# A fused attention and SwiGLU decode step: constant products in the first pass, and the last rows of W_O sent to half of the partitions

## The chip, the cores and the metric

The kernel runs on one core of a Trainium2 chip. The metric is the device time of one launch in microseconds. Before the change three runs gave 196.25, 196.48 and 198.06, so the median is 196.48 us. Lower is better. One further execution was taken with the hardware profiler; it took 196.53 us, of which 195.2 us lie between the first and the last instruction (the span).

## The reference

One decode step for a batch of 4, with one token of width 512 each:

```python
xn  = layernorm(x)                                  # x: 4 x 512
q   = xn @ wq                                       # 32 query heads of 128
k,v = last 4096 positions of the caches             # 8 key/value heads, 4 query heads share one
o   = softmax(q @ k.T * 128**-0.5) @ v
out = x + o @ wo + (silu(xn @ w_gate) * (xn @ w_up)) @ w_down
```

All tensors are bf16. The K and V windows together are 64 MiB, the five weight matrices about 13 MiB, and each byte is used once. The output is 4 x 512.

## The kernel before, in words

Five engines run their own instruction lists, written out by hand and tied by semaphores: TensorE (PE, with its weight loads as PEld), VectorE (DVE), ScalarE (ACT), GpSimd (POOL), and SyncE (SP), which issues all loads but that of x. The order of the loads is the order in which SP issues them: W_Q, W_gate, W_up, then for each of eight passes two halves of K and the whole of V, with W_down behind the first V, and at the end W_O in four pieces. There is one buffer for K, in two halves, and one for V. So a half of K waits until PE has transposed the same half of the pass before (line 264), and a V waits until the products with the V before have ended (line 269).

The start (lines 408 to 445) normalizes x, makes the queries, gate and up products, and ends in 14 constant products (`spin`), which multiply a tile of ones by a constant mask and whose result nobody reads.

A pass r (lines 521 to 539) handles one key/value head for all four batch rows. Each of the 128 partitions holds 128 positions, in 16 chunks of 8. PE transposes a chunk (L451), DVE or ACT copies it out of PSUM (L357, L299), and PE makes the scores two chunks later (L466). DVE then reduces maxima (L363, L365), PE transposes them (`maxima`, L473), DVE makes the shift from them (L368 to L372), PE adds the shift to the scores by a product (`shift`, L478), ACT takes the exponential (L302), and PE makes P·V (L487) and the denominators (L493). The signal that P·V has ended lets SP load the next V and DVE take the sums (L375, L376). `fin` (L500, L502) and `norm` (L380 to L385) of a pass run inside the next one. Between scores and maxima stand five constant products, between maxima and shift five, and behind P·V four, each group under `eng.If(r > 0)`, so that the first pass skips them.

The tail (lines 541 to 568) finishes the last pass, multiplies by W_down, and then by W_O. W_O lies with 32 rows on each partition: partition p holds rows 32p to 32p + 31. The attention result has another layout, with head dimension and quarter spread over the partitions, so four products with a selecting matrix `dr` (L551) permute it and DVE copies the result to OP (L401). The pieces of W_O are rows 0 to 21, 22 to 26, 27 to 29 and 30 to 31 of every partition (`WOS`). The first 22 rows go through `acc4` (L507), four rows side by side into four strips of PSUM, whose sums ACT copies to SBUF (L314) and PE adds by `acc` (L511) with a selecting matrix. The other rows go straight through `acc`, four products of 128 columns for a row. DVE and ACT copy the result out (L404, L317), and two stores end the kernel.

Of the kernel before, what the change touches and what calls it, by code (L numbers as in the profile page):

```python
# [10 lines left out]
def bass_parallel_sum__sliding_block_cached__swiglu_ffn__decode_kernel(  # L11
# [32 lines left out]
    SCALE = float(Dh) ** -0.5  # L44
    EPS = 1e-5
    OFF = -1.0e9
    WOS = (0, 22, 27, 30, 32)
    WOE = 22
    NR = HQ * Dh // 128

# [6 lines left out]
    WU = sb("wu_sb", [128, NC, F], BF16, 512)  # L57
    WD = sb("wd_sb", [128, NF, D], BF16, 512)
    WO = sb("wo_sb", [128, NR, D], BF16, 512)
    X = sb("x_sb", [B, D], BF16, 512)  # L60
    KT = sb("kT", [128, 4, CH, 128], BF16, 512)
    Qb = KT[:, 3].rearrange("p (a k) d -> p a (k d)", a=2)
# [22 lines left out]
    OT = sb("oT", [128, B, HKV + 1, REP, 4], BF16)  # L85

    OP = sb("oP", [128, NR, 32], BF16)
    S2 = sb("s2", [128, D], FP32)
    ex = S2[:, 0:F // 4]
    sel4 = sb("sel4", [128, B], FP32)  # L90
# [43 lines left out]
    acc_ps = ps_S[0][:, 0:HD]  # L134
    acc4_ps = ps_S[1]
    perm_ps = ps_kt[2][:, 0:B * NR]

    def sem(name):
        return nc.alloc_semaphore(name=name)
# [3 lines left out]
    d_wu = sem("d_wu")  # L143
    d_wd = sem("d_wd")
    d_out = sem("d_out")
    d_wo = [sem("d_wo%d" % q) for q in range(4)]
    d_k = [sem("d_k%d" % s) for s in range(2)]
    d_v = sem("d_v")
    s_go = sem("s_go")
# [29 lines left out]
    s_nrm = sem("s_nrm")  # L179
    s_pm = sem("s_pm")  # L180
    s_pc = sem("s_pc")
    s_e = sem("s_e")
    s_ec = sem("s_ec")
    s_acc = sem("s_acc")
# [6 lines left out]
    wu_ap = B_w_up.rearrange("(p c) n -> p c n", c=NC)  # L191
    wd_ap = B_w_down.rearrange("(p t) n -> p t n", t=NF)
    wo_ap = A_wo.rearrange("(p r) n -> p r n", r=NR)

    def kv_ap(cache, g, a, b):
        return cache[:, g, Sk - W:, :].rearrange("b (j t) d -> j b t d", j=NJ)[:, :, a:b, :]
# [62 lines left out]
    def on_sync(eng):  # L259
        H = NT // 2  # L260

        def load_k(g, h):
            if g > 0:
                eng.wait_ge(s_tr, NCH * (g - 1) + (h + 1) * NCH // 2)
            eng.dma_start(KB[:, h * H:(h + 1) * H, :], kv_ap(A_k_cache, g, h * H, (h + 1) * H)).then_inc(d_k[h], 16)

        def load_v(g):
            if g > 0:
                eng.wait_ge(s_pv, g)
            eng.dma_start(VB[:], kv_ap(A_v_cache, g, 0, NT)).then_inc(d_v, 16)  # L270

        def load_wo(n, a, b):
            eng.dma_start(WO[:, a:b, :], wo_ap[:, a:b, :]).then_inc(d_wo[n], 16)

        eng.dma_start(WQ[:], wq_ap).then_inc(d_wq, 16)
        eng.dma_start(WG[:], wg_ap).then_inc(d_wg, 16)
        eng.dma_start(WU[:], wu_ap).then_inc(d_wu, 16)
        for g in range(HKV):
            load_k(g, 0)
            load_k(g, 1)  # L280
            load_v(g)
            if g == 0:
                eng.dma_start(WD[:], wd_ap).then_inc(d_wd, 16)
        for q in range(4):
            load_wo(q, WOS[q], WOS[q + 1])
        eng.wait_ge(s_y[0], 1)
        eng.dma_start(out_ap[0], y[:, 0:D // 2]).then_inc(d_out, 16)
        eng.wait_ge(d_out, 32)
# [33 lines left out]
    def on_vector(eng):  # L322
        eng.wait_ge(d_x, 16)
        eng.tensor_reduce(st_sum[:], X[:], AX.X, ALU.add)  # L324
        eng.drain()
        eng.tensor_scalar(st_mean[:], st_sum[:], 1.0 / D, None, ALU.mult)
        eng.drain()
        eng.tensor_scalar(xc[:], X[:], st_mean[:, 0:1], None, ALU.subtract)
        eng.drain()
        eng.tensor_tensor(xsq[:], xc[:], xc[:], ALU.mult)  # L330
        eng.drain()
        eng.tensor_reduce(st_sum[:], xsq[:], AX.X, ALU.add)
        eng.drain()
        eng.tensor_scalar(st_var[:], st_sum[:], 1.0 / D, EPS, ALU.mult, ALU.add).then_inc(s_var, 1)
        eng.wait_ge(s_std, 1)
        eng.reciprocal(st_rstd[:], st_std[:])
        eng.drain()
        eng.tensor_scalar(xn[:], xc[:], st_rstd[:, 0:1], None, ALU.mult).then_inc(s_xn, 1)  # L338
        eng.wait_ge(s_xT, 1)
        eng.tensor_copy(XnT[:, :, 0:B], xT_ps.rearrange("p (c b) -> p c b", b=B)).then_inc(s_xnT, 1)  # L340
        eng.wait_ge(s_zero, 1)
        eng.tensor_copy(sel4b[:], sel4[:])
        eng.wait_ge(s_q, 1)
        eng.tensor_copy(Qb[:, 0], ps_S[0][:]).then_inc(s_qb, 1)
        eng.wait_ge(s_qt, 1)
        for j in range(2):
            eng.tensor_copy(QT[:, 0:HKV].rearrange("p (n j) (b h) -> p j n b h", j=2, b=B)[:, j],
                            qt_ps.rearrange("p (j h) (n b) -> p j n b h", j=2, n=4)[:, j, :, 0:B, :])
        eng.drain()

        eng.tensor_copy(QC[:], QT[:, 0])

        def group(r):
            for c in range(NCH):
                if c not in ACT_CH:
                    eng.wait_ge(s_tr, r * NCH + (c + 1))
                    eng.tensor_copy(KT[:, c % 4], kt_ps[c % 3]).then_inc(s_ev, 1)  # L357
                if c == 2:
                    norm(r)
                for q in range(NB):  # L360
                    if c == min(NCH - 1, (q + 1) * NCH // NB + 1):
                        eng.wait_ge(s_sc, r * NB + (q + 1))
                        eng.tensor_reduce(mx[:, q, :], ps_S[q][:].rearrange("p (t n) -> p n t", n=NH), AX.X, ALU.max)  # L363
            eng.drain()
            eng.tensor_reduce(m16[:], mx[:].rearrange("p q n -> p n q"), AX.X, ALU.max).then_inc(s_m, 1)  # L365
            eng.tensor_copy(QC[:], QT[:, bass.ds(r + 1, 1)].rearrange("p o n -> p (o n)"))
            eng.wait_ge(s_mt, r + 1)
            eng.tensor_tensor(junk[:], mT_ps, moff[:], ALU.add)  # L368
            eng.drain()
            eng.tensor_reduce(M[:], junk[:], AX.X, ALU.max)  # L370
            eng.drain()
            eng.scalar_tensor_tensor(CM[0:NH, :], neg[:], M[:, 0:1], coff[:], ALU.mult, ALU.add).then_inc(s_cm, 1)  # L372

            eng.wait_ge(s_pv, r + 1)
            eng.tensor_copy(Osb[:], O_ps)  # L375
            eng.tensor_reduce(dsum[:], den_ps.rearrange("p (t n) -> p n t", n=NH), AX.X, ALU.add).then_inc(s_dn, 1)  # L376

        def norm(r):
            eng.wait_ge(s_fin, r + 1)
            eng.reciprocal(den[:], D2_ps)  # L380
            eng.drain()
            eng.tensor_tensor(on[:], O2_ps, den[:], ALU.mult)
            eng.drain()
            o = OT[:, :, r] if isinstance(r, int) else OT[:, :, bass.ds(r, 1)].rearrange("p b o h q -> p b (o h) q")
            eng.tensor_tensor(o, on[:].rearrange("p (b h) -> p b h", b=B).unsqueeze(3).to_broadcast([128, B, REP, 4]),  # L385
                              dq[:].unsqueeze(1).unsqueeze(1).to_broadcast([128, B, REP, 4]), ALU.mult).then_inc(s_nrm, 1)

        eng.wait_ge(s_ex, 1)
        eng.tensor_scalar(ex, ex, 1.0, None, ALU.add)
        eng.drain()  # L390
        eng.reciprocal(ex, ex)
        eng.drain()
        eng.tensor_tensor(gs[:], gate_ps, ex, ALU.mult)
        eng.drain()
        eng.wait_ge(s_u, 1)
        eng.tensor_tensor(GUc, up_ps, gs[:], ALU.mult).then_inc(s_gu, 1)
        with eng.Fori(0, HKV) as r:
            group(r)
        norm(HKV)
        eng.wait_ge(s_pm, 1)  # L400
        eng.tensor_copy(OP[:, :, 0:B].rearrange("p r b -> p b r"), perm_ps.rearrange("p (b r) -> p b r", b=B)).then_inc(s_pc, 1)  # L401
        eng.wait_ge(s_acc, 1)
        for n in range(2):
            last = eng.tensor_copy(y[:, HD * n:HD * (n + 1)], acc_ps[32 * n:32 * n + B, :])  # L404
        last.then_inc(s_y[0], 1)

    def on_tensor(eng):
# [113 lines left out]
        with eng.Fori(0, HKV) as r:  # L521
            for c in range(NCH):
                transposes(r, c)
                if c == 2:
                    fin(r)
                if c >= 2:
                    scores(r, c - 2)
            scores(r, NCH - 2)
            scores(r, NCH - 1)
            with eng.If(r > 0):  # L530
                spin(5)
            maxima(r)
            with eng.If(r > 0):
                spin(5)
            shift(r)
            eng.wait_ge(d_v, r * 16 + 16)
            pv(r)
            with eng.If(r > 0):
                spin(4)

        fin(HKV)
        eng.wait_ge(s_gd, 1)
# [6 lines left out]
        eng.wait_ge(s_nrm, HKV + 1)  # L549
        for b in range(B):  # L550
            last = mm(perm_ps[:, NR * b:NR * (b + 1)], OT[:, b, 1:].rearrange("p k h q -> p (k h q)"), dr[:])  # L551
        last.then_inc(s_pm, 1)
        spin(2, 1)
        acc(ident[0:B, 0:B], X[:], True, False)
        eng.wait_ge(s_pc, 1)
        for q in range(4):
            eng.wait_ge(d_wo[q], 16)
            for e in range(WOS[q], WOS[q + 1]):
                if e < WOE:
                    last = acc4(e % 4, OP[:, e, :], WO[:, e, :], False, e >= WOE - 4)  # L560
                else:
                    last = acc(OP[:, e, 0:B], WO[:, e, :], False, e == NR - 1)
            if WOS[q + 1] == WOE:
                last.then_inc(s_e, 1)
            if q == 1:
                eng.wait_ge(s_ec, 1)
                acc(sel4[:], S2[:], False, False)
        last.then_inc(s_acc, 1)


# [34 lines left out]
```

## Time and profile before

| What | Value |
|---|---|
| median of three runs | 196.48 us (196.25 to 198.06) |
| the profiled execution | 196.53 us |
| its span | 195.2 us |
| PE busy | 161.9 us, 83% of the span |
| DVE busy | 108.8 us, 56% |
| ACT busy | 62.7 us, 32% |
| bytes read from HBM | 81.01 MB, 415 GB/s over the span |
| share of the loads' queue in the time of 16 transfer engines | 97.4% |
| mean granted PE clock | 0.956 |

Busy time is a mean over stages. A matmul's end is modelled, so that a busy PE is not PE at its peak. The 16 transfer engines share each load; a load has landed when all its parts have. The granted clock is the share of full speed that PE is given in a stretch of time.

### The profile page before, as it was taken

The numbers are of one execution on the slowest core, as the hardware profiler recorded it, in microseconds if no ns is written. First come the engines' busy times: TensorE is split into PE (matmuls) and PEld (weight loads), VectorE is DVE, ScalarE is ACT, GpSimd is POOL, SyncE is SP. The second block draws the span as 40 slices with busy tenths as digits, with TensorE's granted clock in tenths as the row PEclk, the third lists the DMA queues.
The fourth block names the chain that finished last, engine by engine and source line by source line (L and its number), as shares of the span: only waits on it lengthen the run. The fifth ranks groups of instructions, "written<-read, shape, count | busy, mean of one in ns | idle before, by whom it ended". The sixth has DMA issues, their size and how long they took to land.

```text
span 195.2 us, 7044 instructions
## 1 busy us (share of the span) xinstructions
PE 161.9 (83%) x3016; PEld 125.9 (65%) x3016; DVE 108.8 (56%) x224; ACT 62.7 (32%) x81; POOL 16.1 (8%) x55
## 2 busy tenths in 40 slices
PE   0038599855499999999999899979997999899994
PEld 0023169723499669947984698559855985698542
DVE  0252847831248828863893478347834783578341
ACT  2003106421026244513553064406440644064402
POOL 7763080000000000000000000000000000000000
PEclk9999699978559999999999999999999999999999
DMA  6999999999999999999999999999999999999992
GB/s 215 431 440 432 419 430 440 440 405 440 430 463 430 410 430 403 436 400 430 447 430 396 443 463 430 403 436 457 430 410 433 453 436 403 430 463 430 419 391 94
DMA packets 4638, 81.09 MB, mean 415 GB/s; under 512 B 524, under 2 KB 536, under 8 KB 920
## 3 DMA queue, kind: packets, MB, share of 16 engines
q1 hardware_dynamic: 4616, 81.01, 97.4%
q8 instruction: 4, 0.07, 0.1%
q14 instruction: 2, 0.02, 0.0%
q10 hardware_dynamic: 16, 0.01, 0.0%
HBM read 81.01 MB, written 0.00 MB: 415 GB/s over the span
## 4 chain that ended last, share of the span: by engine, by line
DMA 48%; PE 46%; DVE 3%; issue 1%; SPq 0%; ACT 0%; DVEq 0%
DMA kbuf<-in_A_k_cache_dram 38%; PE ps_kt L451 21%; DMA wu_sb<-in_B_w_up_dram 10%; PE ps_kt L437 7%; PE ps_s L466 6%; PE ps_o L487 3%; PE ps_s L502 2%; DVE kT L357 2%; PE ps_s L478 1%; PE ps_s L507 1%; PE ps_s L500 1%; PE ps_s L432 1%; PE ps_o L493 0%; DVE oP L401 0%; PE ps_s L511 0%
## 5 line engine op out<-in xcount | busy, mean ns | idle before, releaser
L451 PE MATMUL ps_kt<-ident,kbuf 128*128 128x128 bf16 x1024 | 77.7, 223 | 8.7 <-DMA kbuf<-in_A_k_cache_dram 8.7
L357 DVE COPY kT<-ps_kt 128x1024 bf16<-128x1024 bf16 x88 | 57.6, 686 | 23.2 <-PE ps_kt L451 22.2
L451 PEld LDWEIGHTS ps_kt<-ident,kbuf 128*128 128x128 bf16 x1024 | 60.5, 99 | 11.7 <-DMA kbuf<-in_A_k_cache_dram 10.9
L299 ACT ACTIVATE kT<-ps_kt 128x1024 bf16<-128x1024 bf16 x40 | 40.9, 1023 | 72.8 <-PE ps_kt L451 72.8
L466 PE MATMUL ps_s<-qC,kT 128*128 128x16 bf16 x1024 | 44.8, 170 | 3.2 <-DVE kT L357 1.7
L466 PEld LDWEIGHTS ps_s<-qC,kT 128*128 128x128 bf16 x1024 | 37.9, 97 | 4.6 <-DVE kT L357 3.8
L437 PE MATMUL ps_kt<-own,ones 128*128 128x512 bf16 x116 | 29.7, 386 | 0.0
L302 ACT ACTIVATE p<-ps_s 128x512 bf16<-128x512 f32 x32 | 16.5, 603 | 34.7 <-PE ps_s L478 34.7
L363 DVE TENSOR_REDUCE mx<-ps_s 128x16 f32<-128x512 f32 x32 | 22.1, 689 | 6.8 <-PE ps_s L466 4.7
L375 DVE COPY osb<-ps_o 128x256 f32<-128x256 f32 x8 | 3.4, 425 | 28.5 <-PE ps_o L493 28.5
L487 PE MATMUL ps_o<-vbuf,p 128*32 128x256 bf16 x512 | 18.3, 281 | 0.3
L487 PEld LDWEIGHTS ps_o<-vbuf,p 128*32 128x32 bf16 x512 | 14.5, 99 | 5.9 <-ACT p L302 4.5
L437 PEld LDWEIGHTS ps_kt<-own,ones 128*128 128x128 bf16 x116 | 9.5, 98 | 11.2 <-issue 3.0
L493 PE MATMUL ps_o<-p,ones 128*32 128x256 bf16 x64 | 16.2, 279 | 0.0
L412 PE MATMUL ps_kt<-i,xn 4*128 4x4 f32 x4 | 0.6, 254 | 12.5 <-DVE xn L338 12.5
L478 PE MATMUL ps_s<-cm,own 128*128 128x512 bf16 x32 | 9.1, 411 | 1.0 <-DVE cm L372 1.0
L412 PEld LDWEIGHTS ps_kt<-i,xn 4*128 4x128 f32 x4 | 0.6, 208 | 12.5 <-issue 12.5
L493 PEld LDWEIGHTS ps_o<-p,ones 128*32 128x32 bf16 x64 | 6.4, 100 | 0.1
L478 PEld LDWEIGHTS ps_s<-cm,own 128*128 128x128 bf16 x32 | 2.6, 101 | 5.6 <-DVE cm L372 3.4
L502 PE MATMUL ps_s<-sel,osb 128*128 128x16 f32 x36 | 5.8, 275 | 0.0
L502 PEld LDWEIGHTS ps_s<-sel,osb 128*128 128x128 f32 x36 | 5.2, 208 | 0.0
L324 DVE TENSOR_REDUCE st_sum<-x_sb 4x1 f32<-4x512 bf16 x1 | 0.7, 674 | 8.1 <-DMA x_sb<-in_A_x_dram 8.1
(96 smaller groups left out, 78.1 us busy)
## 6 DMA issues: line engine op xcount, KB each, us to landing
kbuf<-in_A_k_cache_dram SPq DMA_DIRECT2D x16, 2048.0 KB, 13.7
vbuf<-in_A_v_cache_dram SPq DMA_DIRECT2D x8, 4096.0 KB, 16.4
wq_sb<-in_A_wq_dram SPq DMA_DIRECT2D x1, 4096.0 KB, 12.8
wo_sb<-in_A_wo_dram SPq DMA_DIRECT2D x1, 2816.0 KB, 22.5
wg_sb<-in_B_w_gate_dram SPq DMA_DIRECT2D x1, 1792.0 KB, 16.3
wu_sb<-in_B_w_up_dram SPq DMA_DIRECT2D x1, 1792.0 KB, 20.1
wd_sb<-in_B_w_down_dram SPq DMA_DIRECT2D x1, 1792.0 KB, 42.4
wo_sb<-in_A_wo_dram SPq DMA_DIRECT2D x1, 640.0 KB, 23.4
```

Of the source, the lines that this page charges most:

```text
L299: eng.activation(KT[:, c % 4], kt_ps[c % 3], ACT.Copy).then_inc(s_ea, 1)
L302: eng.activation(P[:, BT * q:BT * (q + 1), :], ps_S[q][:].rearrange("p (t n) -> p t n", n=NH), ACT.Exp, scale=SCALE).then_inc(s_p, 1)
L357: eng.tensor_copy(KT[:, c % 4], kt_ps[c % 3]).then_inc(s_ev, 1)
L363: eng.tensor_reduce(mx[:, q, :], ps_S[q][:].rearrange("p (t n) -> p n t", n=NH), AX.X, ALU.max)
L375: eng.tensor_copy(Osb[:], O_ps)
L437: mm(ps_kt[k][:], ones[:], own[:].unsqueeze(1).to_broadcast([128, 4, 128]), skip_group_check=True)
L451: last = eng.transpose(kt_ps[c % 3][:, k, :], KB[:, CH * c + k, :], ident[:])
L466: last = mm(ps_S[q][:, NH * t:NH * (t + 1)], KT[:, c % 4, k, :], QC[:], start=(t == 0), stop=False, skip_group_check=True)
L478: mm(ps_S[q][:].rearrange("p (t n) -> p t n", n=NH), own[:], CM[:].unsqueeze(1).to_broadcast([128, BT, NH]), start=False, stop=True, skip_ ...
L487: mm(O_ps[32 * n:32 * n + 32, :], P[:, t:t + 2, :].rearrange("p t n -> p (t n)"), VB[:, t:t + 2, :].rearrange("p t d -> p (t d)"), start=( ...
L493: last = mm(den_ps[32 * n:32 * n + 32, :], ones[:, 0:32], P[:, DT * e:DT * (e + 1), :].rearrange("p t n -> p (t n)"), start=False, stop=(e ...
L502: last = mm(O2_ps, Osb[:, Dh * h:Dh * (h + 1)], sel[:, NH * h:NH * (h + 1)], start=(h == 0), stop=(h == 1), skip_group_check=True)
```

## The change

Two things change. First, the three groups of constant products in a pass lose their condition: the first pass runs them too, and the branches around them go.

Second, the fourth piece of W_O, its rows 30 and 31 of every partition, takes another way. It no longer goes to W_O's tile over 128 partitions by one transfer. It goes to a view of the W_gate tile, which is free by then, on partitions 0 to 63: partition p gets the two rows of the old partition p (h = 0) and the two of the old partition p + 64 (h = 1). Eight transfers bring it, of eight partitions each, every fourth one: 0, 4, ..., 28, then 1, 5, ..., 29, and so on, and then the same from 32 on. They share one semaphore. So that the products find the attention result on the same partitions, PE makes four more permuting products, which bring the values of partitions 64 to 127 for these two rows to partitions 0 to 63, and DVE copies them to a new tile OX. The last eight products over 128 partitions become sixteen over 64.

```diff
-    WOS = (0, 22, 27, 30, 32)
+    WOS = (0, 22, 27, 30)
+    NX = NR - WOS[-1]
+    WX = WG[:].rearrange("p c n -> p (c n)")[:, 0:2 * NX * D].rearrange("p (h r n) -> p h r n", h=2, r=NX)
+    OX = sb("oX", [64, NX, B], BF16)
+    permx_ps = ps_kt[2][0:64, B * NR:B * (NR + NX)]
+    wx_ap = A_wo.rearrange("(h p r) n -> p h r n", h=2, r=NR)[:, :, WOS[-1]:, :]
...
-        for q in range(4):
+        for q in range(3):
             load_wo(q, WOS[q], WOS[q + 1])
+        for a in (0, 32):
+            for b in range(a, a + 4):
+                eng.dma_start(WX[b:a + 32:4], wx_ap[b:a + 32:4]).then_inc(d_wx, 16)
...
         eng.tensor_copy(OP[:, :, 0:B].rearrange("p r b -> p b r"), perm_ps.rearrange("p (b r) -> p b r", b=B)).then_inc(s_pc, 1)
+        eng.tensor_copy(OX[:].rearrange("p r b -> p b r"), permx_ps.rearrange("p (b r) -> p b r", b=B)).then_inc(s_px, 1)
...
-            with eng.If(r > 0):
-                spin(5)
+            spin(5)
             maxima(r)
-            with eng.If(r > 0):
-                spin(5)
+            spin(5)
             shift(r)
             eng.wait_ge(d_v, r * 16 + 16)
             pv(r)
-            with eng.If(r > 0):
-                spin(4)
+            spin(4)
...
         for b in range(B):
             last = mm(perm_ps[:, NR * b:NR * (b + 1)], OT[:, b, 1:].rearrange("p k h q -> p (k h q)"), dr[:])
+            last = mm(permx_ps[:, NX * b:NX * (b + 1)], OT[:, b, 1 + HKV // 2:].rearrange("p k h q -> p (k h q)"),
+                      dr[:, WOS[-1]:])
...
-        for q in range(4):
+        for q in range(3):
...
-                    last = acc(OP[:, e, 0:B], WO[:, e, :], False, e == NR - 1)
+                    acc(OP[:, e, 0:B], WO[:, e, :], False, False)
...
+        eng.wait_ge(s_px, 1)
+        eng.wait_ge(d_wx, 8 * 16)
+        for e in range(NX):
+            acc(OP[0:64, WOS[-1] + e, 0:B], WX[0:64, 0, e, :], False, False)
+            last = acc(OX[:, e, :], WX[0:64, 1, e, :], False, e == NX - 1)
         last.then_inc(s_acc, 1)
```

More of the change, by code (lines that the diff above doesn't have):

```diff
@@ L145, in bass_parallel_sum__sliding_block_cached__swiglu_ffn__decode_kernel @@
     d_out = sem("d_out")
-    d_wo = [sem("d_wo%d" % q) for q in range(4)]
+    d_wo = [sem("d_wo%d" % q) for q in range(3)]
+    d_wx = sem("d_wx")
     d_k = [sem("d_k%d" % s) for s in range(2)]
@@ L181, in bass_parallel_sum__sliding_block_cached__swiglu_ffn__decode_kernel @@
     s_pc = sem("s_pc")
+    s_px = sem("s_px")
     s_e = sem("s_e")
```

## The prediction

> **What bounds the kernel now.** I read the page first, then the chain of work that ended last, then the transfers and the clock by stretches. The page gives the frame.
>
> ```profile
> span 195.2 us, 7044 instructions
> ...
> DMA  6999999999999999999999999999999999999992
> ...
> q10 hardware_dynamic: 16, 0.01, 0.0%
> ```
>
> The transfer engines are busy from the second slice to the last but one, so what counts is bytes, and after them the short tail behind the last byte. (Forty equal slices; a 9 is 90% or more.) The q10 row is used below. Next the chain, its last part, for pass 7 and the tail.
>
> ```profile
> 51.39 2.74 PE ps_kt L451 x24
> ...
> 110.13 1.51 PE ps_kt L451 x24
> ...
> 168.42 1.51 PE ps_kt L451 x24
> ...
> 189.32 0.21 PE ps_kt L551 x4
> 189.56 0.72 DVE oP L401
> 190.32 1.49 PE ps_s L507 x22
> 191.84 0.60 ACT s L314
> 192.49 0.70 PE ps_s L511 x28
> 193.21 0.28 DVE y_sb L404
> ```
>
> Columns: start, length, what. PE starts pass 7 at 168.42, when the first half of its K lands, and from there to the end the chain holds no transfer: transposes, scores, softmax, P·V, then permutation (L551), its copy (L401), W_O products (L507), the copy of partial sums (L314), the last products (L511) and the output. So the end is the landing of that K plus some 25 us of engine work. The same rows show where a delay came from: passes 4 to 7 start 3 apart in (168.42 - 110.13) = 58.29 us, while the three before took 110.13 - 51.39 = 58.74. The earlier three lost 0.45 us.
>
> The last W_O transfer must be compared with that chain. These rows are the transfers' issues (size, time to landing), W_O's issue instruction (min/median/max ns, first and last start), and stretches of the tail (the last two columns are the share of the 16 transfer engines and GB/s).
>
> ```profile
> wo_sb<-in_A_wo_dram SPq DMA_DIRECT2D x1, 384.0 KB, 23.9
> wo_sb<-in_A_wo_dram SPq DMA_DIRECT2D x1, 256.0 KB, 24.1
> ```
>
> ```profile
> L273 SPq DMA_DIRECT2D wo_sb<-in_A_wo_dram x4: 432/432/600, 167.1 to 168.7; - x4
> ```
>
> ```profile
> 189.60:190.20 0.60, 0.51 (x6) 0.09 (x4) 0.60 (x1) 0.00 (x0) 0.00 (x0) 1.00 1.00 408
> ...
> 190.80:191.40 0.60, 0.60 (x16) 0.28 (x12) 0.00 (x0) 0.00 (x0) 0.00 (x0) 1.00 0.80 304
> ...
> 192.00:192.40 0.40, 0.08 (x4) 0.00 (x0) 0.00 (x0) 0.40 (x1) 0.00 (x0) 1.00 0.07 26
> ```
>
> The last transfer was issued at 168.7 and landed 24.1 us later, at 192.8. The engines do not finish together: the share sinks over 1.5 us, and 0.07 of sixteen engines after 192.0 is one engine alone, the **straggler**.
>
> ```profile
> 189.25 0.27 PE L551 MATMUL ps_kt<-dr,oT 128*128 128x32 bf16 x4
> ...
> 192.71 0.46 PE L511 MATMUL ps_s<-wo_sb,oP 128*4 128x128 bf16 x20
> ```
>
> ```profile
> L511 PE MATMUL ps_s<-wo_sb,oP 128*4 128x128 bf16 x40 | 1.1, 219 | 0.0
> ...
> L551 PE MATMUL ps_kt<-dr,oT 128*128 128x32 bf16 x4 | 0.3, 180 | 0.0
> ```
>
> The second pair groups the tail by line (busy us, mean ns of one). Of the 20 products from 192.71, the last eight use the last two rows. With 219 ns for one, the starts are (0.46 - 0.22)/19 = 0.0126 us apart, so the thirteenth starts at 192.86: some 0.06 us after the landing. PE is the bound here, the straggler close behind.
>
> **The change part by part, first the constant products in pass 0.** PE alone in and behind pass 0, then the chain in pass 1 for the same steps with constant products, then the clock by stretches (second column from the left after the times is PE busy; the third from the right is the granted clock).
>
> ```profile
> 38.93 0.52 PE L466 MATMUL ps_s<-qC,kT 128*128 128x16 bf16 x15 [0.76 <-issue]
> 40.57 0.22 PE L473 MATMUL ps_kt<-ident,m 128*16 128x128 bf16 x1 [1.12 <-DVE m L365]
> 41.81 1.89 PE L478 MATMUL ps_s<-cm,own 128*128 128x512 bf16 x4 [1.02 <-DVE cm L372]
> ...
> 46.26 0.27 PE L493 MATMUL ps_o<-p,ones 128*32 128x256 bf16 x1
> 51.39 1.89 PE L451 MATMUL ps_kt<-ident,kbuf 128*128 128x128 bf16 x16 [4.86 <-DMA kbuf<-in_A_k_cache_dram]
> ```
>
> ```profile
> 57.67 0.87 PE ps_kt L451 x8
> ...
> 60.15 0.46 PE ps_kt L451 x8
> ...
> 66.01 0.36 PE ps_s L466 x8
> 66.37 1.09 PE ps_kt L437 x5
> ...
> 72.00 0.97 PE ps_kt L437 x4
> ```
>
> ```profile
> 41.80:45.20 3.40, 3.38 (x36) 1.61 (x40) 0.00 (x0) 2.06 (x4) 0.00 (x0) 0.50 1.05 443
> 45.20:48.60 3.40, 1.33 (x48) 0.97 (x40) 0.76 (x2) 0.00 (x0) 0.00 (x0) 1.00 0.96 413
> 48.60:52.00 3.40, 0.61 (x6) 0.61 (x7) 0.00 (x0) 0.00 (x0) 0.00 (x0) 0.50 1.02 439
> 52.00:58.90 6.90, 6.90 (x87) 6.90 (x85) 3.55 (x8) 1.35 (x2) 0.00 (x0) 0.50 1.00 432
> ```
>
> ```profile
> 72.00:76.00 4.00, 4.00 (x65) 3.53 (x66) 3.08 (x8) 0.37 (x1) 0.00 (x0) 1.00 1.03 401
> 76.00:100.00 24.00, 23.61 (x500) 20.27 (x498) 17.08 (x34) 10.90 (x13) 0.00 (x0) 1.00 1.01 429
> ```
>
> The fourteen products stand where PE waited 1.12 us for the maxima and 1.02 us for the shift, and behind P·V. At full clock five take 1.09 us and four 0.97, so the first two groups fill the waits almost exactly. The stretch from 41.8 ran at half clock after those waits; filled, it should run at full clock. Pass 1, with products, needs 72.00 - 66.37 = 5.63 us from its last scores to the end of P·V; pass 0 ends its scores at 39.45, so P·V would end near 45.1 instead of 46.53. That moves one transfer, V of pass 1, which SP holds until P·V has ended:
>
> ```profile
> 46.59 0.54 SPq L270 DMA_DIRECT2D vbuf<-in_A_v_cache_dram  x1
> ...
> 72.04 0.54 SPq L270 DMA_DIRECT2D vbuf<-in_A_v_cache_dram  x1
> ```
>
> Issued 1.4 us earlier it still stands behind both halves of K, the first of which lands only at 51.39. Gain: 0. PE then idles from about 45.1 + 0.97 = 46.05 to 51.39, 5.3 us instead of 4.86, and I expect it cold again at 51.39: already the 1.33 us of work in 45.20 to 48.60 left the next stretch at half clock. So pass 1 stays as it is, its P·V ends at 72.0, and V of pass 2 is issued at 72.04, too late: 401 GB/s in 72 to 76 against 429 after. That is the 0.45 us lost above, and it stays. The branches that go cost nothing in later passes, since the products follow the scores directly (66.01 + 0.36 = 66.37).
>
> The Trainium skill, "TensorE: Matmul & The Clock Gate", section on HAM oscillation, says that a wait longer than a window of 3.4 us takes the clock back to half, which speaks against a use of these products for pass 1; the wait of 4.86 us ahead of 51.39, with a clock of 0.50 behind it, agrees. Without that rule the second rival below would have more weight, and its 196.3 with it.
>
> **The W_O rows.** (a) PE, permutation: four more products, narrower. Starts of the four are (0.27 - 0.18)/3 = 0.03 us apart; four more, between the others, cost 0.12. Bounds: 0 (if they slip into the pipeline) and 4 x 0.07. They stand on the chain ahead of the copy at 189.56: +0.12. (b) DVE, the second copy: no row; the nearest, 4 x 128 out of PSUM, takes 0.28. It stands behind the signal for the first copy, beside 1.49 us of W_O products: 0; it would cost its 0.28 only if the first copy waited for it. (c) PE, last products: two rows in halves of 64 are sixteen instead of eight: 8 x 0.0126 = +0.10; bounds 0.05 and 0.2. Two waits in place of one: the copy is done by about 190.8, long before, so 0, at most 0.06. (d) SP: eight issues for one, 8 x 0.43 to 0.60 = 3.5 to 4.8 us from 168.6 on; what is queued ahead keeps the transfer engines busy to 190, so 0; behind them SP only waits for the output. (e) The bytes are the same 256 KB. The q10 row bounds their spread: its 16 packets are two transfers of four partitions (x and half of the output), eight packets each, four of data and four that close an engine's share, so four engines worked. With eight partitions I take eight engines. One engine moves 408/16 = 25.5 GB/s; 32 KB instead of 16 is 0.64 us more on those eight, 0.64 less on the others. Eight closings in place of one: the landings 384 to 256 KB stand 0.53 + 0.2 = 0.7 apart, 0.64 of it bytes, so 0 to 0.06 each; I take 0, since 189.6 to 190.2 shows no loss between transfers.
>
> Where do these land? All engines but the straggler are done by about 192.3, so those of the eight end by 192.3 + 0.64 = 192.9 at worst. PE reaches them at 192.86 + 0.12 = 192.98. PE stays the bound, and freeing the straggler gains nothing.
>
> The Trainium skill, "DMA: Bandwidth & Descriptors", in the section on why a semaphore rises by 16, says that the number of engines is the largest up to 16 that divides the slowest dimension of both sides, the lowest-numbered ones: eight here, which the q10 row agrees with. Its rules for kernel authors speak against the change: two transfers to disjoint halves spray over all engines anyway; by that the straggler would keep its share, land at 192.8, and the sum would be the same.
>
> Sum: +0.12 + 0.10 = **+0.22 us**. The profiled execution took 196.53 us (195.2 of span, 1.33 around), near the median of 196.48. 196.53 + 0.22 = **196.75**.
>
> **The rivals.** *Slower, the straggler is one of the eight.* Nothing in the page names the engine. Then it lands 0.64 later, at 193.4, against PE's 192.98, and the end moves by 0.45 more: 197.2. It decides once one of the eight ends the transfer before later than 192.98 - 1.28 = 191.7; the straggler ends it at 192.8 - 0.64 = 192.16. For: half of the engines are chosen. Against: the other half too. *Faster, the dip at 72 to 76 goes.* If constant products keep or bring the clock back earlier in pass 1 (its eight transposes take 0.87 us cold, 0.46 warm), P·V of pass 1 ends over a microsecond sooner and the 0.45 us come back: 196.3. Against it stands the idle time before 51.39. *The clock comes back later.* The clock changes in steps of 3.4 us that do not follow the kernel's start; one more cold step in pass 1 is at most 3.4 x (1 - 0.46/0.87) = 1.6 us on V of pass 2, nearly all visible behind the dip: 198.3, close to the highest run of before (198.06). *The change does not do what it says:* the transfers spread over all engines; as forecast.
>
> **How the numbers follow.** Forecast 0.62 (with the last rival; its own range 196.4 to 197.1 by the bounds of a to e), slower straggler 0.15, dip gone 0.13, later clock 0.10. The range leaves out the last and the rims: 196.1 to 197.4. One per cent, about what a measurement of this kernel can tell from no change, is 194.5 to 198.4: faster 0.02, within 0.93, slower 0.05, from the later clock's upper rim.
>
> **What would show it.** In the profile after: the clock at full from 41.8; P·V of pass 0 ends near 45.1; PE idles over 5 us before pass 1 and starts it at half clock; V of pass 2 is issued near 72; the copy of the permutation starts 0.12 us later against the preceding product; sixteen last products without a transfer as their releaser; a DMA share of about a half once the last transfer but one is done. I am wrong if pass 1 starts warm, or if PE waits for the eight transfers at the end.

## The result, and the profile after

The changed kernel takes 197.11 us (median of 22 runs, 196.96 to 199.6). The kernel before, in 22 runs beside it, takes 196.47 (195.87 to 198.06). The ratio is 1.0051, with a 95% interval of 1.0028 to 1.0074: slower by 0.55 to 1.45 us, and the medians differ by 0.64. I had forecast +0.22. The sign was right and the time lies in the range, but the size was a third of what the medians show.

The profiled execution took 198.47 us. It is one of the longer runs (its span is 197.1, while 14 of the 22 runs have one of 195.6 to 196.3), so a part of what its rows show belongs to this run alone, and the experiments are needed to part the two. First the row of the loads' queue from the page of the profile:

```profile
q1 hardware_dynamic: 4664, 81.01, 96.4%
```

The same queue in the kernel before:

```profile
q1 hardware_dynamic: 4616, 81.01, 97.4%
```

The bytes are the same, and there are 48 more packets. The data need 128 packets in either form: 128 partitions by one of 2 KB, or eight transfers by eight partitions by two. So the small packets that close an engine's share went from 16 to 64, that is eight for each transfer: eight engines each, as predicted. The end of the chain (start, length, what):

```profile
173.41 21.16 DMA wg_sb<-in_A_wo_dram
194.57 0.14 issue
194.70 0.42 PE ps_s L524 x16
...
195.15 0.28 DVE y_sb L417
```

Before, the chain held PE alone from the start of pass 7. Now it ends with a landing, at 194.57, and behind it the sixteen last products. The issue at 173.41 doesn't cause this: the engines are busy with earlier bytes until 190.2, so the transfer stands in the queue for most of its 21.16 us. The timeline of the tail, ahead of it the start of pass 7 (start, length, engine, line, operation; in brackets the idle time before and what ended it):

```profile
167.94 1.51 PE L464 MATMUL ps_kt<-ident,kbuf 128*128 128x128 bf16 x24 [0.96 <-DMA kbuf<-in_A_k_cache_dram]
...
188.77 0.19 PE L561 MATMUL ps_kt<-dr,oT 128*128 128x32 bf16 x1
...
188.89 0.19 PE L562 MATMUL ps_kt<-dr,oT 128*64 128x2 bf16 x1
...
189.62 0.19 PE L562 MATMUL ps_kt<-dr,oT 128*64 128x2 bf16 x1
...
189.85 0.71 DVE L413 CAST oP<-ps_kt 128x128 bf16<-128x128 f32 x1 [1.94 <-PE ps_kt L562]
190.20 0.36 DVE L414 CAST oX<-ps_kt 64x8 bf16<-64x8 f32 x1
...
193.00 0.35 PE L524 MATMUL ps_s<-wo_sb,oP 128*4 128x128 bf16 x12
...
194.70 0.22 PE L524 MATMUL ps_s<-wg_sb,oP 64*4 64x128 bf16 x4 [1.35 <-DMA wg_sb<-in_A_wo_dram]
```

Two things stand here. PE waits 1.35 us for the eight transfers. And the eight permuting products, four wide (L561, 128 weight columns) in turns with four narrow (L562, 64), start 0.12 us apart: from the first to the copy 189.85 - 188.77 = 1.08 us pass, where before it was 189.56 - 189.25 = 0.31. That is +0.77, and my sum had +0.12. The transfer engines at the end (time, busy time of PE, PEld, DVE, ACT and POOL, granted clock, share of the 16 engines, GB/s):

```profile
190.20:190.80 0.60, 0.48 (x9) 0.21 (x12) 0.36 (x2) 0.00 (x0) 0.00 (x0) 1.00 0.86 335
...
192.40:193.00 0.60, 0.22 (x9) 0.21 (x12) 0.00 (x0) 0.33 (x1) 0.00 (x0) 1.00 0.06 17
193.00:193.80 0.80, 0.35 (x20) 0.16 (x8) 0.00 (x0) 0.00 (x0) 0.00 (x0) 1.00 0.06 21
```

A share of 0.06 is one engine alone, for 1.4 us and more. Four packets of 2 KB on it took 200 to 232 ns, where 84 is the median; no other profile of the eight transfers has such a packet. The landing comes 194.57 - 167.94 = 26.6 us behind the start of pass 7, where the five other profiles of kernels with the eight transfers have 24.8 to 25.3. So what makes this run long is its landing. Last the first pass: PE and SP by time, and the clock by stretches.

```profile
40.23 0.52 PE L479 MATMUL ps_s<-qC,kT 128*128 128x16 bf16 x15 [0.62 <-issue]
...
46.34 1.04 PE L450 MATMUL ps_kt<-own,ones 128*128 128x512 bf16 x4
51.48 1.78 PE L464 MATMUL ps_kt<-ident,kbuf 128*128 128x128 bf16 x16 [4.11 <-DMA kbuf<-in_A_k_cache_dram]
```

```profile
46.45 0.53 SPq L279 DMA_DIRECT2D vbuf<-in_A_v_cache_dram  x1
...
71.90 0.54 SPq L279 DMA_DIRECT2D vbuf<-in_A_v_cache_dram  x1
```

```profile
41.80:45.20 3.40, 3.33 (x48) 1.70 (x50) 0.88 (x5) 1.64 (x4) 0.00 (x0) 1.00 1.04 435
...
52.00:58.90 6.90, 6.90 (x89) 6.90 (x88) 3.58 (x8) 1.37 (x2) 0.00 (x0) 0.53 1.01 437
72.00:76.00 4.00, 4.00 (x69) 3.63 (x68) 3.12 (x8) 0.51 (x1) 0.00 (x0) 1.00 1.05 418
```

The clock is full from 41.8 (it was 0.50), PE idles 4.11 us ahead of pass 1, and pass 1 runs at half clock again (0.53). V of pass 2 is issued at 71.90 (before: 72.04).

### The profile page after: what moved, and what is told of

The parts are those of the page before. It is cut to its first block, busy times and chain, and to the rows that moved or that the text cites. A ratio compares the mean times of both kernels' runs of the same rounds, so it can differ in the third digit from the quotient of the medians.

```text
span 197.1 us, 7081 instructions
## 1 busy us (share of the span) xinstructions
PE 165.9 (84%) x3042; PEld 127.4 (65%) x3042; DVE 108.8 (55%) x225; ACT 62.7 (32%) x81; POOL 15.9 (8%) x55
## 4 chain that ended last, share of the span: by engine, by line
DMA 51%; PE 40%; SPq 4%; DVE 2%; issue 2%; DVEq 0%
DMA kbuf<-in_A_k_cache_dram 30%; PE ps_kt L464 19%; DMA wg_sb<-in_A_wo_dram 11%; DMA wu_sb<-in_B_w_up_dram 10%; PE ps_kt L450 7%; PE ps_s L479 6%; PE ps_o L500 3%; SPq L297 2%; DVE kT L369 2%; PE ps_s L515 2%; PE ps_s L491 1%; PE ps_s L445 1%; SPq L282 1%; PE ps_s L513 1%; PE ps_o L506 0%
## 5 line engine op out<-in xcount | busy, mean ns | idle before, releaser
L450 PE MATMUL ps_kt<-own,ones 128*128 128x512 bf16 x130 | 34.7, 399 | 0.0
L450 PEld LDWEIGHTS ps_kt<-own,ones 128*128 128x128 bf16 x130 | 11.0, 101 | 13.6 <-issue 5.2
L500 PE MATMUL ps_o<-vbuf,p 128*32 128x256 bf16 x512 | 17.6, 274 | 0.3
L491 PE MATMUL ps_s<-cm,own 128*128 128x512 bf16 x32 | 8.3, 380 | 0.0
```

The source lines that it names most:

```text
L450: mm(ps_kt[k][:], ones[:], own[:].unsqueeze(1).to_broadcast([128, 4, 128]), skip_group_check=True)
L491: mm(ps_S[q][:].rearrange("p (t n) -> p t n", n=NH), own[:], CM[:].unsqueeze(1).to_broadcast([128, BT, NH]), start=False, stop=True, skip_ ...
L500: mm(O_ps[32 * n:32 * n + 32, :], P[:, t:t + 2, :].rearrange("p t n -> p (t n)"), VB[:, t:t + 2, :].rearrange("p t d -> p (t d)"), start=( ...
```

## The experiments

**The two parts alone.** First the constant products without the W_O rows, that is the kernel before with the three conditions taken away:

```diff
-            with eng.If(r > 0):
-                spin(5)
+            spin(5)
...
-            with eng.If(r > 0):
-                spin(4)
+            spin(4)
```

> The kernel before with the constant products also in the first pass, W_O as before. Theory A (the products keep the clock through the first passes, and the loss between the end of pass 1 and the start of pass 2 goes): 0.3 to 0.6 us faster than before, near 196.0, with a mean granted clock near 0.99. Theory B (the products change nothing, since PE idles until K of pass 1 lands): as before, 196.5, with the same spread.

Measured: 196.51 us (195.99 to 198.88), beside 196.46 for before; ratio 0.9985 [0.9951, 1.0018]. No change, as forecast. Then the W_O rows with the conditions kept, that is the changed kernel with the three put back:

```diff
-            spin(5)
+            with eng.If(r > 0):
+                spin(5)
...
-            spin(4)
+            with eng.If(r > 0):
+                spin(4)
```

> The changed kernel with the products of the first pass skipped again, so W_O's rows alone are changed. If the rows cost what the changed kernel's trace shows on PE (permutation to its copy 1.08 us in place of 0.31, so 0.77, and 0.1 for the last products), it is 0.9 us slower than before, 197.4; if theory A holds for the products it is also 0.3 to 0.6 us slower than the changed kernel. If theory B holds it is as the changed kernel, 197.1.

Measured: 198.24 us (196.95 to 199.84); ratio 1.0076 [1.0039, 1.0113]. So the loss comes from the W_O rows. The median is above the 197.1 to 197.4 that was expected; its runs spread over nearly 3 us. The interval overlaps that of the whole change, and whether the products give part of it back is not settled by these two runs.

The profiled execution of the products alone was the longest of its runs, and shows what made it long: the clock and the issue of V of pass 2.

```profile
52.00:60.80 8.80, 8.80 (x110) 8.80 (x109) 4.81 (x9) 2.05 (x2) 0.00 (x0) 0.50 1.05 452
72.00:76.00 4.00, 4.00 (x79) 3.27 (x70) 2.32 (x5) 0.19 (x1) 0.00 (x0) 1.00 0.98 365
```

```profile
73.02 0.53 SPq L270 DMA_DIRECT2D vbuf<-in_A_v_cache_dram  x1
```

Half clock holds until 60.8 instead of 58.9, V is issued 1.0 us later than in the profile of before, and 72 to 76 moves 365 GB/s instead of 401. This is the rival of the later clock, by its own mechanism. It is not what made the changed kernel's profiled run long: there V was issued at 71.90, and pass 7 started at 167.94, earlier than in the profile of before (168.42).

**The order of the permuting products.** The changed kernel with the same products, the four narrow ones behind the four wide ones:

```diff
         for b in range(B):
             last = mm(perm_ps[:, NR * b:NR * (b + 1)], OT[:, b, 1:].rearrange("p k h q -> p (k h q)"), dr[:])
+        for b in range(B):
             last = mm(permx_ps[:, NX * b:NX * (b + 1)], OT[:, b, 1 + HKV // 2:].rearrange("p k h q -> p (k h q)"),
                       dr[:, WOS[-1]:])
```

> The changed kernel with the four full permutation products first and the four narrow ones behind them, instead of in turns. Theory P (what costs is the change between full and narrow weights, seven times 0.09 us): the stretch from the first permutation product to its copy falls from 1.08 to 0.4 to 0.6 us, and the time falls by 0.4 to 0.7 where PE is the bound. Theory D (the landing of the eight transfers is the bound): the stretch falls too, but PE then waits longer for the transfers and the time stays within 0.2 us of the changed kernel.

```profile
188.99 0.27 PE L561 MATMUL ps_kt<-dr,oT 128*128 128x32 bf16 x4
...
189.18 0.29 PE L563 MATMUL ps_kt<-dr,oT 128*64 128x2 bf16 x4
...
189.50 0.71 DVE L413 CAST oP<-ps_kt 128x128 bf16<-128x128 f32 x1 [1.39 <-PE ps_kt L563]
```

Measured: 197.68 us (196.75 to 199.71), ratio 1.0049 [1.0012, 1.0086]. First product to copy is 0.51 us instead of 1.08, so the turns cost 0.57. But the lowest time falls by 0.2 only (196.96 to 196.75), and the median doesn't tell. What stands right behind is the landing of the eight transfers: the trace has the last at 192.94, and the first product that needs it starts at 193.08, while the last product ahead of it had started at 192.79.

**One transfer instead of eight**, to 64 partitions, in the changed kernel and in the one with grouped products:

```diff
-        for a in (0, 32):
-            for b in range(a, a + 4):
-                eng.dma_start(WX[b:a + 32:4], wx_ap[b:a + 32:4]).then_inc(d_wx, 16)
+        eng.dma_start(WX[0:64], wx_ap).then_inc(d_wx, 16)
...
-        eng.wait_ge(d_wx, 8 * 16)
+        eng.wait_ge(d_wx, 16)
```

> The changed kernel with one transfer of 64 partitions in place of eight of eight partitions; PE's work is the same. Theory D: no wait ahead of the sixteen last products, the landing some 0.7 to 1.5 us earlier, and the time 0.5 us or more below the changed kernel. Theory P: the landing is earlier as well, but PE comes to it late, so the lower end of the runs stays at 197.0 and only the slow runs above 197.5 get rarer.

> The changed kernel with the permutation products in two groups and one transfer of 64 partitions in place of eight. If the alternation (0.57 us of it gone in the grouped kernel's trace) and the late landing of the eight transfers right behind it are together what the rows cost, both go here, and what is left is the prediction's 0.2 to 0.3 us: the lowest runs at 196.2 to 196.4, the median 196.5 to 196.9. If something else of the rows costs as much (the two waits, the halves of 64 partitions), the lowest runs stay at 196.7 or above.

Measured: 197.37 us (196.93 to 198.32), ratio 1.0033 [1.0003, 1.0064], and 197.27 (196.73 to 199.56), ratio 1.004 [1.0, 1.008]. Neither is told apart from the eight transfers. The 0.5 us less that the first might have shown did not come, and with both edits the lowest run stayed at 196.73, where 196.2 to 196.4 was expected if turns and late landing were the whole cost. With both edits PE waits for the landing, which comes at 193.10 (chain, then timeline, of the run with both):

```profile
168.13 24.96 DMA wg_sb<-in_A_wo_dram
```

```profile
193.23 0.22 PE L522 MATMUL ps_s<-wg_sb,oP 64*4 64x128 bf16 x4 [0.25 <-DMA wg_sb<-in_A_wo_dram]
```

In these two profiles the transfers slowed down between 190.0 and 191.7: of the 128 packets of 3 KB, 20 and 19 took 205 to 376 ns there instead of 121. Why was not tried, so these two runs don't say what one transfer would be worth without that.

**What spaces the products.** In the kernel before, in the loop of L551, four more products in turns with the four permuting ones, whose result nobody reads. First with 64 weight columns:

```diff
+            last = mm(ps_kt[2][0:64, 128 + 2 * b:130 + 2 * b], OT[:, b, 1 + HKV // 2:].rearrange("p k h q -> p (k h q)"),
+                      dr[:, 30:])
```

and then with 128:

```diff
+            last = mm(ps_kt[2][:, 128 + 2 * b:130 + 2 * b], OT[:, b, 1:].rearrange("p k h q -> p (k h q)"),
+                      dr[:, 30:])
```

> The kernel before with the four narrow permutation products (weights of 64 columns) put between the full ones, their result unread; W_O, its transfers and the products of the first pass as before. Theory P: the stretch from the first permutation product to the copy is 1.08 us in place of 0.31, and the lowest runs rise from 195.9 to 196.6 or 196.7. If the alternation costs only beside the other changes: 195.9 to 196.1.

> The same with weights of 128 columns in the four added products, moving two columns as before; nothing reads them. If the change of the weights' width is what spaces the products, the starts stay 0.03 us apart, the stretch is 0.4 to 0.45 us and the lowest runs are at 196.0 to 196.1. If it is the change of the moving operand, or the turns as such, the starts are 0.12 us apart and the stretch is about 1.08 again, as in the kernel with 64 columns.

The timeline with 64 columns:

```profile
190.87 0.19 PE L551 MATMUL ps_kt<-dr,oT 128*128 128x32 bf16 x1
...
190.99 0.19 PE L552 MATMUL ps_kt<-dr,oT 128*64 128x2 bf16 x1
...
191.95 0.72 DVE L401 CAST oP<-ps_kt 128x128 bf16<-128x128 f32 x1 [1.94 <-PE ps_kt L552]
```

and with 128:

```profile
189.78 0.19 PE L551 MATMUL ps_kt<-dr,oT 128*128 128x32 bf16 x1
...
189.97 0.16 PE L552 MATMUL ps_kt<-dr,oT 128*128 128x2 bf16 x1
...
190.17 0.72 DVE L401 CAST oP<-ps_kt 128x128 bf16<-128x128 f32 x1 [1.26 <-PE ps_kt L552]
```

First product to copy: 1.08 us with 64 columns, 0.39 with 128 (and 0.31 without any). The eight products start 0.12 us apart in the one case, and (189.97 - 189.78)/7 = 0.027 in the other. Turns and moving operand are the same, so what costs is the change between 128 and 64 weight columns. The times agree at their lowest: 196.60 against 195.91, and 195.91 for before beside them; the medians, 196.89 (ratio 1.001 [0.9976, 1.0043]) and 196.45 (0.9983 [0.9952, 1.0014]), don't decide. The Trainium skill, "TensorEngine Tiling (Array Packing)", section "Tiling Modes", says that changing the tiling mode drains TensorE, and lists 128x64 as a mode of its own. The spacing agrees; that it is a drain no run shows.

**Filling the wait ahead of pass 1.** The runs of all these kernels spread over 2 to 4 us, which hides differences of 0.2. If the spread comes from the clock after the wait of 4 to 5 us, constant products in that wait should remove it. In the kernel with the products alone, 18 more behind P·V of the first pass:

```diff
             spin(4)
+            with eng.If(r < 1):
+                spin(18)
```

> The kernel before with the constant products also in the first pass, and 18 more behind the first pass's four, so that PE is busy for 3.9 us more of the 5.3 us that it waits for K of pass 1; W_O as before. Theory of the clock (the slow runs and the loss before pass 2 come from a half clock in pass 1): pass 1 starts at full clock, V of pass 2 is issued before 70, nearly all runs lie between 195.9 and 196.3, and the median is 0.3 to 0.5 us below before. If the slow runs come from elsewhere: median 196.4 and the same spread as before.

```profile
48.14 4.92 PE L437 MATMUL ps_kt<-own,ones 128*128 128x512 bf16 x22
52.90 1.50 PE L451 MATMUL ps_kt<-ident,kbuf 128*128 128x128 bf16 x24
```

```profile
52.00:58.90 6.90, 6.90 (x137) 6.39 (x136) 4.83 (x10) 2.05 (x2) 0.00 (x0) 1.00 1.03 442
...
72.00:76.00 4.00, 4.00 (x92) 4.00 (x90) 3.49 (x8) 1.78 (x2) 0.00 (x0) 1.00 1.05 451
```

Measured: 196.06 us (195.78 to 196.30), ratio 0.9941 [0.9915, 0.9967]: faster than before (the changed kernel did not run beside it), and twelve runs within 0.52 us. Pass 1 starts late, at 52.90 (before: 51.39), because the products last longer than the wait (the first half of K had landed at 51.6), but it starts at full clock, and the dip at 72 to 76 is gone (451 GB/s against 401). V of pass 2 is issued at 70.36, not quite before 70 as the theory had it. This is the mechanism of the rival that I called *the dip goes*, which the change itself did not bring about. The Trainium skill, "TensorE: Matmul & The Clock Gate", section on HAM oscillation, says that a wait longer than its window takes the clock down. Both sides agree with it: a wait of 4.11 us and a clock of 0.53 behind it in the changed kernel, the wait filled and a clock of 1.00 here.

The same with the conditions kept, so that the first pass has only 22 products behind P·V:

```diff
             with eng.If(r > 0):
                 spin(4)
+            with eng.If(r < 1):
+                spin(22)
```

> The kernel before with its conditions kept, and 22 constant products behind P·V of the first pass. If the 4.86 us wait ahead of pass 1 is all that the clock needs filled, as with all products: 196.0 to 196.2, all runs close together, no half clock behind the wait. If the products between scores, maxima and shift matter too, the stretch from 41.8 is at half clock, pass 1 starts no later than with them, and the time lies between 196.1 and 196.5.

```profile
48.60:52.00 3.40, 3.40 (x21) 1.64 (x19) 0.00 (x0) 0.00 (x0) 0.00 (x0) 1.00 1.02 429
52.00:58.90 6.90, 6.90 (x157) 6.90 (x155) 5.50 (x11) 3.07 (x3) 0.00 (x0) 1.00 1.03 442
```

Measured: 196.06 us (195.80 to 197.44), ratio 0.9974 [0.9943, 1.0006]. The median is the same and pass 1 is at full clock, but two of the twelve runs lie a microsecond above the rest and the interval takes in 1. That the wait alone has to be filled is likely, not shown.

**The W_O rows with the wait filled.** Three kernels: the changed one with the 18 products, the same with the permuting products grouped, and the same with the narrow ones widened to 128 columns, of whose results the upper half is not read. The last one's edit (the products stay in turns, and oT gets a row of zeros at its end):

```diff
-    permx_ps = ps_kt[2][0:64, B * NR:B * (NR + NX)]
+    permx_ps = ps_kt[2][:, B * NR:B * (NR + NX)]
...
-            last = mm(permx_ps[:, NX * b:NX * (b + 1)], OT[:, b, 1 + HKV // 2:].rearrange("p k h q -> p (k h q)"),
+            a = (b * (HKV + 1) + 1 + HKV // 2) * REP * 4
+            last = mm(permx_ps[:, NX * b:NX * (b + 1)], OT[:].rearrange("p b k h q -> p (b k h q)")[:, a:a + 128],
```

> The changed kernel with 18 further constant products behind P·V of the first pass. Theory: with the wait ahead of pass 1 filled, the clock stays up, the runs lie close together, and what is left above the unchanged W_O with the same products (196.06) is the price of the W_O rows alone: 0.77 us of permutation instead of the 0.12 forecast, 0.1 of last products, 0.1 to 0.2 of landing: 197.0 to 197.1. Rival: the rows cost what I forecast, and the rest came from the clock: 196.3.

> As the run before this one, with the four narrow permuting products behind the four wide ones instead of in turns with them. If only PE's permutation were late, it gives back 0.57 us: 196.4. If the landing of the eight transfers stands right behind, about 0.2 us: 196.7 to 196.9.

> As the first run of this call, with the four added permuting products made 128 weight columns wide (the results of the upper 64 are not read), still in turns with the others. Theory (the change of width between products spaces them): first product to copy takes 0.4 us instead of 1.08, and the time is that of the grouped form, 196.6 to 196.9, held there by the landing. Rival (the turns, or reading other columns of the same tile, space them): 1.08 us and 197.0 as without the edit.

| Kernel, wait filled, 12 runs each | median, us | ratio to before | span, median | span, lowest to highest |
|---|---|---|---|---|
| W_O as before | 196.06 | 0.9941 [0.9915, 0.9967] | 194.8 | 194.5 to 195.1 |
| rows, in turns | 197.80 | 1.0043 [1.0016, 1.0069] | 195.7 | 195.5 to 196.0 |
| rows, grouped | 196.88 | 1.0013 [0.9988, 1.0038] | 195.55 | 195.1 to 196.0 |
| rows, widened | 196.89 | 0.9988 [0.9959, 1.0017] | 195.6 | 195.1 to 195.7 |

The spans are as close as hoped, and are the ones to compare, since the time of the rows in turns holds something else: what lies outside the span was 1.2 to 2.4 us in its runs (median 2.1), against 1.2 to 1.5 in all the others shown here. No run tells why, and its time of 197.80 stands against 197.0 to 197.1 expected for that reason alone: 195.7 and the usual 1.3 are 197.0.

The first row ran on another chip than the three below it; the kernel with only the 22 products, which ran on the chip of those three, has the same median span, 194.8.

By spans the rows cost 0.9 us. The profiles show where. The end of the chain with W_O as before:

```profile
168.02 1.51 PE ps_kt L451 x24
...
192.09 0.70 PE ps_s L511 x28
192.81 0.28 DVE y_sb L404
```

and with the rows in turns, chain and timeline:

```profile
167.84 1.51 PE ps_kt L464 x24
...
192.68 0.92 PE ps_s L524 x36
193.62 0.28 DVE y_sb L417
```

```profile
188.67 0.19 PE L563 MATMUL ps_kt<-dr,oT 128*128 128x32 bf16 x1
...
189.75 0.71 DVE L413 CAST oP<-ps_kt 128x128 bf16<-128x128 f32 x1 [1.94 <-PE ps_kt L564]
...
192.90 0.35 PE L524 MATMUL ps_s<-wo_sb,oP 128*4 128x128 bf16 x12
...
193.18 0.22 PE L524 MATMUL ps_s<-wg_sb,oP 64*4 64x128 bf16 x4
```

From the start of pass 7 to the first output copy it is 192.81 - 168.02 = 24.79 us without the rows (24.79 in the profile of before too, 193.21 - 168.42) and 193.62 - 167.84 = 25.78 with them: +0.99. Of that 0.77 is the permutation (189.75 - 188.67 = 1.08 again) and 0.92 - 0.70 = 0.22 the last products. No transfer stands in this chain, but one stands right beside it. The trace has the last of the eight landings at 193.025, between the twelve products from 192.90 and the first of the sixteen at 193.18, 0.15 us ahead of that. In the seven other profiles with the new rows, be it by eight transfers or by one, the first of the sixteen starts 0.135 to 0.137 us behind the last landing. So here products and landing are equally late, within 0.02 us. The timelines of the widened form, and then of the grouped one:

```profile
167.86 1.51 PE L465 MATMUL ps_kt<-ident,kbuf 128*128 128x128 bf16 x24 [1.01 <-DMA kbuf<-in_A_k_cache_dram]
...
188.69 0.19 PE L564 MATMUL ps_kt<-dr,oT 128*128 128x32 bf16 x1
...
189.08 0.71 DVE L414 CAST oP<-ps_kt 128x128 bf16<-128x128 f32 x1 [1.25 <-PE ps_kt L566]
...
193.30 0.22 PE L525 MATMUL ps_s<-wg_sb,oP 64*4 64x128 bf16 x4 [0.72 <-DMA wg_sb<-in_A_wo_dram]
```

```profile
193.15 0.22 PE L524 MATMUL ps_s<-wg_sb,oP 64*4 64x128 bf16 x4 [0.53 <-DMA wg_sb<-in_A_wo_dram]
```

With 128 columns the permutation takes 0.39 us in the changed kernel as well, which settles the width as its cause. PE then waits 0.72 us (grouped: 0.53) for the eight transfers, so the 0.69 us won at the permutation are nearly all lost again: by the spans 0.1 to 0.15 us is left. The landing is a second bound, as late as the spaced products: with the permutation only 0.08 us longer than before, the rows still cost 0.8 us (spans of 195.6 against 194.8).

## Why the prediction was right or wrong

Two steps failed, and either one alone would have cost most of what was measured: the price of the permutation in (a), and the landing in (e), from which I concluded that PE stays the bound.

**Where it failed first: (a), the permutation.** Its bounds were 0 and 4 x 0.07 us, and I took 0.12. It is 0.77. The starts 0.03 us apart came from four products of one shape, and the new ones were priced at that row with the word "narrower" as if it could only help. No row of before showed a product of 128 columns next to one of 64 that closely, and I had bounded the unseen operation by the seen one instead of by a whole product: eight times the 0.18 us of one, less the 0.31, would have given an upper end above 1 us. The kernel before with four narrow products added has this cost alone: 1.08 us instead of 0.31, and a lowest time of 196.60 against 195.91.

**Where it failed second: (e), the landing.** The eight transfers use eight engines, as predicted, but land later: I had them done at 192.9 at worst, 24.48 us behind the start of pass 7 at 168.42. In the widened form PE goes on at 193.30, which is 25.44 us behind its pass 7, and 0.14 of that lies between landing and product: 25.3, later by 0.8. That PE waits for the eight transfers at the end was my own sign of being wrong, and it came (1.35 us in the profile after, 0.72 and 0.53 in the widened and grouped forms). One part is the price of the closings, which I put at 0. On the engine that ends last in the widened form the packets that close the eight shares end 0.166 us apart, but its last three landings are 0.20 apart, so the landings fall behind. The last landing comes 0.66 us behind the last data (192.50 and 193.16), where in the profile of before it was 0.33 (192.43 and 192.75). The other part, some 0.5 us, is data that came later than forecast: the last of it 24.64 us behind the start of pass 7, and 24.14 to 24.61 in the four other profiles with the eight transfers and spans of 195.5 or 195.6, against 24.01 before. What makes it late is not told apart. Of the two places of the Trainium skill, "DMA: Bandwidth & Descriptors", that the prediction cites, the section on why a semaphore rises by 16 agrees with the 64 closings. Its rule for kernel authors on two halves, which spray over all engines, does not carry over to transfers of eight partitions.

**Right in mechanism, too small: (c).** The last products cost 0.22 instead of 0.10, just outside the bounds of 0.05 and 0.2. Eight more starts are 0.11; the rest is a gap ahead of the first product over 64 partitions, where I had allowed 0.06 for the second wait. The landing falls into that gap, so it need not be a price of PE's own. The two waits may have a part: where PE waits for a landing, its product starts 0.045 us behind it with one wait (the kernel before with the four added products of 128 columns), and 0.135 to 0.137 with two. Whether the wait or the change from 128 to 64 partitions makes this difference is open.

**Right: (b) and (d).** The second copy (0.36 us) is hidden. SP's eight issues take 5.9 us, 0.67 to 0.83 each instead of 0.43 to 0.60, and are hidden behind the queue.

**The first pass.** The clock is full from 41.8, and the products alone change nothing (0.9985 [0.9951, 1.0018]): right. P·V ends near 46.4 and not at 45.1, but the scores also ended later, at 40.75, and 40.75 + 5.63 is 46.4. The idle time was 4.1 us instead of 5.3 and the clock still fell, so V of pass 2 is issued at 71.90 where I said near 72.

**The rivals.** *Slower, the straggler is one of the eight* came nearest to the time, 197.2, and its end is what the profiles show: the landing comes last, or level with PE. Its reason is not shown, since no row names the engine, and a span of 195.6 to 195.8, which most runs have, does not tell the two bounds apart: the rows in turns, where they are level, and the widened form, where PE waits, both have it. That the measured time lies in the range is owed to this rival, not to the forecast's own sum, whose bounds ended at 197.1. *Later clock* made the profiled run of the products alone long, and filling the wait took most of the spread away; the changed kernel's profiled run was long by its landing. *The dip goes* needs the wait filled. Summed anew, 0.77 + 0.22 gives +0.99 for PE's chain, where the lowest times differ by 196.96 - 195.87 = 1.09. The medians differ by 0.64 only, since more runs of before lie above its lowest (its median by 0.60, that of the changed kernel by 0.15); whether the products do that is open, as the runs of each part alone didn't show it.

## What to carry to other kernels

An operation that the profile doesn't show in that neighbourhood is bounded by its whole length, not by the spacing of its like. Keep matrix products of one weight width together, or pad the narrow ones to the wide form: four padded products cost 0.08 us here, and four narrow ones in turns 0.77. And before a step on the path is made shorter, look for what lands right behind it: the 0.69 us won here met a transfer after 0.15. A landing is not the last byte either: with eight small transfers it came 0.65 us and more behind the data, with one over 128 partitions about 0.3.

## What the runs showed of the hardware

- Where products of 128 and of 64 weight columns came in turns, their starts were 0.12 us apart; without a change of width they were 0.027 apart.
- Filling a wait of about 5 us with constant products kept the granted clock at 1.00 through the pass behind it. With the products in all three places it narrowed the runs from a spread of 2 us and more to 0.5 us and took 0.59% [0.33%, 0.85%] off the time, although pass 1 began 1.5 us later.
- Transfers of eight partitions occupy eight engines, with 64 closing packets for eight transfers. Each is issued in 0.67 to 0.83 us, longer than one of 128 partitions (0.43 to 0.60).
- With eight such transfers the last landing came 0.65 to 0.85 us behind the last data in the six profiles that have them; with one transfer over 128 partitions it was 0.28 to 0.35 in six, with one over 64 it was 0.39 and 0.42.
- The time outside the span can differ by 0.8 us between kernels that differ only in the order of four products, for a reason that nothing here shows.
